# Token DFT of a fused spectral and mixer block: two pairs of row blocks moved from the plain first columns into the first group of the second half, and the first half's results summed in DRAM

## The chip, the cores and the metric

The kernel runs on one core of one Trainium2 chip. The metric is the device time of one execution in microseconds (us). Three runs of the kernel before gave 871.83, 871.90 and 871.99 us, median 871.9 us. TensorE (PE) does the matrix multiplications, VectorE (DVE) and ScalarE (ACT) do elementwise work, GpSimd (POOL) and SyncE (SP) here only issue DMAs, apart from a few small fills.

## What is computed

```python
xn = _layernorm(x, axis=-1)                       # x: 2048 tokens x 640 channels
a = jnp.einsum("bsd,ed->bse", xn, dft_hid_re)
b = jnp.einsum("bsd,ed->bse", xn, dft_hid_im)
y = jnp.einsum("ts,bse->bte", dft_seq_re, a) - jnp.einsum("ts,bse->bte", dft_seq_im, b)
...
h = _layernorm(xn, axis=-1)
u = _gelu(jnp.einsum("bsd,sf->bdf", h, w1) + b1)  # mixed over tokens
return x + y + (jnp.einsum("bdf,fs->bds", u, w2) + b2).transpose(0, 2, 1)
```

The kernel does the DFT over the tokens first and the one over the channels behind it. Everything is in float32.

## The kernel before

**The order of the whole.** There are four stages on PE: the DFT over the tokens, the DFT over the channels ("hid"), and the two matrices of the mixer ("up", "down"). The change is in the first stage, which runs to 403 us in the profile.

**The token DFT.** The 2048 tokens are 16 blocks of 128 rows, k = 0 to 15. The two DFT matrices (m = 0 real, m = 1 imaginary) are read from DRAM in pieces of 128 rows by 512 columns (c = 0 to 3). A matmul takes 128 rows by 128 channels of the normalized x as the stationary operand and a piece of a matrix as the moving one, and sums in one of PE's eight PSUM banks. Float32 accuracy is had from a split: each operand is a high part (`high`, L139, on ACT) and a low part, the rest (`low`, L142, on DVE), and each product is three matmuls (high x high, high x low, low x high; `three`, L150, L151 and L153). The two halves of the split of one piece are called its cut here.

**Plain columns and groups.** The rows come in two halves, h = 0 (blocks 0 to 7) and h = 1 (blocks 8 to 15). The columns c = 0 of the first half are done plainly (`first_columns`, L460): 8 row blocks, 2 matrices, 5 blocks of 128 channels and 3 passes, 240 matmuls on L479. They can start before all rows are there. Every other pair of a half and a column chunk is a group (`columns`, L538), g = 0 to 6: g = 0, 1, 2 are columns 1, 2, 3 of the first half, g = 3 is column 0 of the second half, g = 4, 5, 6 its columns 1, 2, 3. In a group the row blocks are taken in four pairs (q and q + 4), the two matrices and four of the five channel blocks form a 2 by 2 block product, and seven products with sums of the operands take the place of eight (a Strassen scheme); the fifth channel block is done plainly. A pair of row blocks takes 7 x 2 x 3 + 4 x 3 = 54 matmuls in a group and 60 plainly.

**Steps and turns.** The work of PE is a list of steps, each with one piece of a matrix. In a group they come as (product, pair), in the order 1, 2, 5, 6, then 3, 7, 3, 4 with product 3 split in two; products 1, 2, 5 and 3 have 9 matmuls in a step, products 6, 7 and 4 have 6. `turn_of(i)` (L1111) writes out what belongs to step i, and every engine runs its own instructions in that order:

```python
for f in loads.pop(i, ()): ...        # SP: pieces of later steps
for f in reads.pop(i, ()): ...        # PSUM banks read out
steps[j][0]()                         # j = i + 2: high part of a later piece, ACT
extras, timed                         # sums of pieces (DVE), others
do_jobs(ahead, short)
ready[j] = steps[j][1]()              # its low part, DVE
do_jobs(behind)
steps[i][2](ready.pop(i))             # the matmuls of step i, PE
```

So what is put in turn i ahead of a cut delays the cut of step i + 2. There are three places for cut pieces, so that the high part of step j also waits for the matmuls of step j - 3. `jobs` is a list of small pieces of work. How many of them a turn takes, ahead of the low part and behind it, is written out by hand (`JOBS_AT`, by the turn's place in its group).

**The first rows.** The seven products need sums of row pieces. `sums_of_rows` (L299) gives them as six jobs for each pair of the first half: job 1 a sum (L312) and a high part, job 2 a low part, a difference and a high part, job 3 and job 4 the like, job 5 a high part, job 6 a low part. The high parts run on ACT, all else on DVE. The start itself is the string `START` of words: x and b load a row block or a piece, M, A, R, I, F and O make the mean and the factors of a row block (DVE, with one square root on ACT), H and L write the high and low part of its normalized channels (`first_rows`, L343), N normalizes the whole row in place (ACT), T and B are the two halves of a cut, P the matmuls of a step.

**Reading out.** Seven of a group's ten result tiles come in two parts (C11, C12 and C22, two tiles each, and the first F). `fresh` (L601) copies a bank to one of six places "c" on ACT (L604); `more` (L609) later adds a second bank to the copy on DVE (L616); then `store_y` (L454) stores the tile to `y_part` in DRAM from POOL's queue, plainly (L456) in the first half and with an adding DMA (L458) in the second. The plain columns are read on L487.

Of the kernel before, what the change touches and what calls it, by code (L numbers as in the profile page):

```python
# [8 lines left out]
F32 = mybir.dt.float32  # L9
# [5 lines left out]
P = 128  # L15
# [18 lines left out]
BLOCK = 18  # L34


FIRST = (
    [(0, 0, 0, 5), (1, 0, 0, 3), (0, 1, 0, 5), (1, 1, 0, 3)] + [(0, k, 0, 5) for k in range(2, 8)]
    + [(1, k, 0, 5) for k in range(2, 8)] + [(1, 0, 3, 5), (1, 1, 3, 5)]
)  # L40

FIRST_AT = [0, 6, 1, 7, 2, 3, 4, 5, 0, 1, 2, 3, 4, 5, 0, 1, 6, 7]
# [11 lines left out]
GROUP = 28  # L54
# [16 lines left out]
def fnet_plus_mixer(  # L71
# [271 lines left out]
    def first_rows(k, which):  # L343
# [103 lines left out]
    c_turn = [5]  # L447
# [6 lines left out]
    def store_y(h, m, c, j, t):  # L454
        if h == 0:
            nc.gpsimd.dma_start(y_part[m][c][:, j, :], t)  # L456
        else:
            nc.gpsimd.dma_start(y_part[m][c][:, j, :], t, accum_op=ALU.add)  # L458

    def first_columns():  # L460
# [10 lines left out]
        def products(w, m, k, j0, j1, passes=(0, 1, 2)):  # L471

            for n in passes:
                rows, cols = ((0, 0), (0, 1), (1, 0))[n]
                for j in range(j0, j1):
                    begin, end = (2, 1) if m == 1 and j >= 3 else (0, 7)
                    if n == 0 and k == begin:
                        banks[m, j] = psum[(5 * m + j) % 8]
                    nc.tensor.matmul(  # L479
                        banks[m, j], channels(k, j)[rows], w[cols], start=n == 0 and k == begin,  # L480
                        stop=n == 2 and k == end, skip_group_check=True,
                    )

        def read(m, js):
            for j in js:
                c = c_tile()
                nc.scalar.activation(c, banks[m, j], AF.Copy)  # L487
                store_y(0, m, 0, j, c)
# [9 lines left out]
        for i in range(14, 16):  # L498
            loads[i - 6].append(lambda i=i: load(i))

        def row(k):
            if k == 0:
                nc.sync.dma_start(x_in[0][:, :H2], x_rows[0][:, :H2])
            else:
                nc.sync.dma_start(x_in[k], x_rows[k])

# [11 lines left out]
        def rooted(k, to=None):  # L518
            ks = slice(k, (to or k) + 1)
            vq[k] = root(mv[:, ks, 1])  # L520

        def inverted(k, to=None):
            inverse(norm[:, 0, k : (to or k) + 1], *vq[k])

        def factored(k, to=None):
            inverted(k, to)
            offset(norm, slice(k, (to or k) + 1))

        return {
            "x": row, "b": load, "e": later_load, "T": top, "B": bottom, "P": run,  # L530
# [7 lines left out]
    def columns(g, h, c):  # L538

        s0 = len(steps)  # L540
        raw = [pieces[(g + m) % 2] for m in range(2)]
        banks, cs = {}, {}

        def load(name, q):
            i, m = int(name[1]) - 1, int(name[2]) - 1
            nc.sync.dma_start(raw[m][:, i, q, :], dft_seq[m * NC + c, 8 * h + q + 4 * i])

        for name, at in (("B11", (-6, -5, -5, -4)), ("B21", (-3, -3, -2, -2)), ("B12", (-2, -1, 0, 0)), ("B22", (1, 2, 3, 4))):
            for q in range(4):
                loads[s0 + at[q]].append(lambda name=name, q=q: load(name, q))  # L550

        def b(name, q, n=1):
            t = raw[int(name[2]) - 1][:, int(name[1]) - 1]
# [3 lines left out]
        order = [(i, q) for i in (1, 2, 5, 6) for q in range(4)]  # L557
        order += [(3, 0), (3, 1)] + [(7, q) for q in range(4)] + [(3, 2), (3, 3)] + [(4, q) for q in range(4)]
        operand = {1: "B11", 2: "B21", 5: "B11", 6: "B11", 3: "B22", 7: "B12", 4: "B21"}
        for names, at in (  # L560
            (("B11", "B12", "B11"), (5, 7)), (("B12", "B22", "B12"), (6, 8)), (("B11", "B22", "B11"), (9, 11)),
            (("B21", "B21", "B11"), (16, 17)),
        ):
            for e in range(2):
                extras[s0 + at[e]].append(lambda names=names, e=e: sub(*(b(n, 2 * e, 2) for n in names)))
# [8 lines left out]
        def products(i, q):  # L574
            def run(w):
                a = fixed[h][q]
# [3 lines left out]
                if i in fifth_of:  # L580
                    m, low_rows = fifth_of[i]
                    first = q == 0 and i in (1, 2)
                    if first:
# [3 lines left out]
                        first, q == 3,  # L587
                    )
                if i in bank_of:
                    for e in range(2):  # L590
                        at = slot[i] * Q + e * P
                        three(
                            banks[bank_of[i], e], (a[:, 0, at : at + P], a[:, 1, at : at + P]), w,
                            q == 0 and i in (1, 2, 5), q == 3,
# [6 lines left out]
        def fresh(name, at, key, e, then=None):  # L601
            def run():
                cs[name, e] = c_tile()
                nc.scalar.activation(cs[name, e], banks[key, e], AF.Copy)  # L604
                if then:
                    store_y(h, *then, cs[name, e])
            reads[s0 + at].append(run)

        def more(name, at, key, e, then):  # L609
# [580 lines left out]
```

## Time and profile before

| what | value |
|---|---|
| median of three runs | 871.9 us |
| time of the profiled execution | 871.46 us |
| its span, first to last instruction | 869.7 us |
| PE busy | 863.2 us, 99% of the span |
| DVE busy | 698.1 us, 80% |
| ACT busy | 516.7 us, 59% |
| mean granted TensorE clock | 0.999 |

A busy time is the time in which an engine had an instruction under way. In a timeline a row has its start, its duration, the engine, the line of the code, the operation with its tiles ("n" is the fixed parts of the rows, "piece" a cut piece, "pieces" the raw ones, "c" a tile that is read out), a count where several rows are merged, and in brackets the idle time ahead of it with what ended it. Instructions that follow each other on DVE or ACT overlap by about 0.1 us, so that the distance of two starts is what one costs in a busy queue.

### The profile page before, as it was taken

The page shows a single profiled execution, that of the slowest core. Times are in us where ns is not written, and L with a number is a line of the kernel's source. Part 1 is how long each engine was busy: PE and PEld are TensorE (multiplying, and loading weights), DVE is VectorE, ACT ScalarE, POOL GpSimd, SP SyncE. Part 2 cuts the span into 40 slices and gives each one's busy share as a digit, 9 for nine tenths or more (in the row PEclk, how much of TensorE's full clock was granted, in tenths as well). Part 3 has the DMA queues.
Part 4 walks back from the last instruction along what each step waited for, and adds up shares of the span by engine and source line. Part 5 has one row for each costly group of instructions (what it writes and reads, how often), then busy time and mean ns, then how long its engine had stood idle before and what let it go on. Part 6 is the DMA issues. An engine that isn't in the chain of part 4 may idle for free.

```text
span 869.7 us, 13949 instructions
## 1 busy us (share of the span) xinstructions
PE 863.2 (99%) x4908; PEld 791.4 (91%) x4908; DVE 698.1 (80%) x1205; ACT 516.7 (59%) x952; POOL 136.0 (16%) x182
## 2 busy tenths in 40 slices
PE   9999999999999999999999999999999999999997
PEld 6888888888888888889999999999999999999997
DVE  7878878785877887877877788888678978897886
ACT  6654666745455555547565556676677866555653
POOL 0110100101120201222110101111322321111211
PEclk9999999999999999999999999999999999999999
DMA  7670644619383755869576756655588788756776
GB/s 289 232 268 35 206 187 149 256 62 357 51 228 65 177 127 131 215 93 188 131 167 167 159 136 204 188 175 153 154 177 187 166 222 236 181 132 133 165 172 128
DMA packets 87270, 148.95 MB, mean 171 GB/s; under 512 B 8672, under 2 KB 37088, under 8 KB 86944
## 3 DMA queue, kind: packets, MB, share of 16 engines
q1 hardware_dynamic: 64784, 95.64, 34.0%
q0 software_dynamic: 22128, 52.18, 31.1%
q8 instruction: 38, 0.62, 0.3%
q14 instruction: 32, 0.26, 0.1%
q10 hardware_dynamic: 288, 0.25, 0.1%
HBM read 99.96 MB, written 53.31 MB: 176 GB/s over the span
## 4 chain that ended last, share of the span: by engine, by line
PE 99%; DMA 0%; DVE 0%; issue 0%; DVEq 0%; ACT 0%
PE psum L151 31%; PE psum L150 31%; PE psum L153 30%; PE psum L479 6%; DMA x<-in_x 0%; DVE st L211 0%; DVE pair L872 0%; DVE r L229 0%; DVEq L1186 0%; DVE mv L214 0%; ACT q L221 0%; DVE norm L233 0%; DVE r L227 0%; DVE v L220 0%; DVE norm L236 0%
## 5 line engine op out<-in xcount | busy, mean ns | idle before, releaser
L142 DVE TENSOR_TENSOR piece<-pieces,piece 128x512 fp32r<-128x512 f32 (+4 forms) x504 | 332.5, 661 | 135.1 <-ACT piece L139 131.4
L139 ACT ACTIVATE piece<-pieces 128x512 fp32r<-128x512 f32 (+2 forms) x480 | 300.4, 626 | 227.5 <-PE psum L153 148.4
L153 PE MATMUL psum<-piece,n 128*128 128x512 f32 x504 | 196.3, 389 | 0.0
L151 PE MATMUL psum<-piece,n 128*128 128x512 f32 x504 | 196.3, 389 | 0.0
L150 PE MATMUL psum<-piece,n 128*128 128x512 f32 x504 | 196.2, 389 | 0.0
L150 PE MATMUL psum<-sdown,piece 128*128 128x320 f32 x392 | 121.0, 310 | 0.0
L151 PE MATMUL psum<-sdown,piece 128*128 128x320 f32 x392 | 120.9, 309 | 0.0
L151 PE MATMUL psum<-sup,piece 128*128 128x320 f32 x392 | 120.9, 309 | 0.0
L150 PE MATMUL psum<-sup,piece 128*128 128x320 f32 x392 | 120.9, 309 | 0.0
L145 DVE TENSOR_TENSOR pieces<-pieces 128x512 f32<-128x512 f32 (+3 forms) x142 | 111.8, 792 | 2.7
L153 PE MATMUL psum<-sup,piece 128*128 128x320 f32 x368 | 113.9, 309 | 0.0
L153 PE MATMUL psum<-sdown,piece 128*128 128x320 f32 x368 | 113.9, 309 | 0.0
L150 PEld LDWEIGHTS psum<-piece,n 128*128 128x128 f32 x504 | 94.7, 188 | 19.7
L151 PEld LDWEIGHTS psum<-piece,n 128*128 128x128 f32 x504 | 94.6, 188 | 19.7
L153 PEld LDWEIGHTS psum<-piece,n 128*128 128x128 f32 x504 | 94.6, 188 | 19.4
L151 PE MATMUL psum<-shid,piece 128*128 128x320 f32 x280 | 86.6, 309 | 0.0
L150 PE MATMUL psum<-shid,piece 128*128 128x320 f32 x280 | 86.6, 309 | 0.0
L153 PE MATMUL psum<-shid,piece 128*128 128x320 f32 x280 | 86.6, 309 | 0.0
L150 PEld LDWEIGHTS psum<-sdown,piece 128*128 128x128 f32 x392 | 73.6, 188 | 0.2 <-issue 0.2
L151 PEld LDWEIGHTS psum<-sdown,piece 128*128 128x128 f32 x392 | 73.6, 188 | 0.0
L151 PEld LDWEIGHTS psum<-sup,piece 128*128 128x128 f32 x392 | 73.6, 188 | 0.0
L150 PEld LDWEIGHTS psum<-sup,piece 128*128 128x128 f32 x392 | 73.6, 188 | 0.0
(113 smaller groups left out, 1101.8 us busy)
## 6 DMA issues: line engine op xcount, KB each, us to landing
pieces<-in_dft_seq SPq DMA_DIRECT2D x128, 256.0 KB, 5.4
pieces<-in_w SPq DMA_DIRECT2D x88, 256.0 KB, 3.7
y<-c POOLq DMA_DIRECT2D x84, 256.0 KB, 6.5
out<-pair POOLq DMA_DIRECT2D x38, 320.0 KB, 5.2
pieces<-y SPq DMA_DIRECT2D x32, 320.0 KB, 4.1
pieces<-in_w SPq DMA_DIRECT2D x32, 192.0 KB, 2.5
out<-in_x SPq DMA_DIRECT2D x16, 320.0 KB, 7.4
up<-pair POOLq DMA_DIRECT2D x8, 640.0 KB, 3.2
```

The lines of the kernel that those rows point to most:

```text
L139: nc.scalar.activation(hi, src, AF.Copy)
L142: nc.vector.tensor_sub(lo, src, hi.bitcast(F32))
L145: nc.vector.tensor_sub(to, a, b)
L150: nc.tensor.matmul(psum, wh, mh, start=first, stop=False, skip_group_check=True)
L151: nc.tensor.matmul(psum, wh, ml, start=False, stop=last and wl is None, skip_group_check=True)
L153: nc.tensor.matmul(psum, wl, mh, start=False, stop=last, skip_group_check=True)
L479: nc.tensor.matmul(banks[m, j], channels(k, j)[rows], w[cols], start=n == 0 and k == begin, stop=n == 2 and k == end, skip_group_check=True,)
```

## The change

Two pairs of row blocks, (2, 6) and (3, 7), are left out of the plain columns. `FIRST` has 10 steps now, with the blocks 0, 1, 4 and 5; the group of the second half's column 0 (g = 3) takes six pairs, its own four and these two, in 42 steps, the pieces of the two more pairs in a tile of their own ("more"). The row blocks 2, 3, 6 and 7 are still normalized and split, since the groups 0 to 2 need them, but blocks 2 and 3 in fewer channels (`first_rows`), and blocks 6 and 7 partly in the turns 10 to 13.

The results of the first half's groups are no longer added on DVE: both parts are copied on ACT, and the second one is stored with an adding DMA (`by_dram`). That is seven additions a group, for g = 0, 1, 2.

The turns are written out from turn 6 on, where the word list ends. The jobs have a new order and new places: turns 6 and 7 take two jobs each, turns 8 and 9 none, and the 28 turns of the first group up to 23. The mean and variance of the later rows become jobs, and these rows are loaded in turns 10, 14, 18 and 22.

```diff
-BLOCK = 18
+BLOCK = 10
+APART = 2
+FIRST_STEP = 6
...
+FIRST = [
+    (0, 0, 0, 5), (1, 0, 0, 3), (0, 1, 0, 5), (1, 1, 0, 3), (0, 4, 0, 5), (0, 5, 0, 5), (1, 4, 0, 5), (1, 5, 0, 5),
+    (1, 0, 3, 5), (1, 1, 3, 5),
+]
...
 START = """
-    x0 b0 x1 b1 b2 x2 b3 x3 b4 x4 x5 b5 x6 x7 b6 b7
+    x0 b0 x1 b1 b2 x4 b3 x5 b4 x2 x3 b5 x6 x7 b6 b7
     M0 A0 R0 T0 I0 D0 O0 H0 B0 N0 T1 M1 A1 R1 L0 T2 B1 F1 H1 P0-0-1 P1-0 P0-2 P1-1-2
-    M2 A2 R2 N1 B2 F2 L1 b8 T3 H2 M3 A3 B3 N2 T4 R3 P2
-    L2 B4 b9 P3 F3 H3 T5 M4 A4 N3 M5 A5 R4-5 B5 F4-5 L3 b10 e0 P4
-    M6 A6 H4 T6 N4 B6 L4 b11 P5 H5 M7 A7 R6-7 T7 N5 B7 F6-7 L5 b12 e1 P6
-    H6 T8 M8 A8 N6 B8 L6 b13 P7 H7 T9 M12 A12 N7 B9 L7
+    M4 A4 R4 N1 B2 F4 L1 T3 H4 M5 A5 B3 N4 T4 R5 P2
+    L4 B4 P3 F5 H5 T5 M2 A2 N5 M3 A3 R2-3 B5 F2-3 L5 q4 P4
+    H2 T6 N2 M6 A6 B6 L2 q5 P5 H3 T7 N3 M7 A7 R6-7 B7 F6-7 L3
 """
...
 JOBS_AT = (
-    ((0, 1, 2, 3, 4, 10, 13, 15, 18, 19, 20, 21, 22, 23, 26, 27), (0, 1, 2, 3), ()),
-    ((0, 1, 2, 3, 4, 19, 22, 27), (), (10, 14, 21)),
+    jobs_at((0, 1, 2, 4, 10, 12, 13, 14, 15, 16, 17, 18, 23, 25, 27), (2, 4, 10, 15, 16, 16, 17, 17)),
+    jobs_at((0, 1, 2, 3, 4, 10, 12, 13, 14, 15, 18, 19, 20, 21, 22, 23, 26, 27), (0, 1, 2, 3)),
+    jobs_at((0, 1, 2, 41)),
+    jobs_at((0, 1, 2, 3, 4, 13, 18, 19, 22, 27), (), (10, 14, 21)),
 )
...
+        if APART <= k < 4:
+            whole[0] = (lambda which: part(a, which, 0), x_in[k][:, :Q])
...
+            late_begin = 4
+            js = (range(3), range(3, 5)) if (m, k) == (1, late_begin) else (range(j0, j1),)
+            for n, j in ((n, j) for part in js for n in passes for j in part):
...
-        reads[10].append(lambda: read(0, range(ND)))
-        reads[16].append(lambda: read(1, range(3)))
-        reads[18].append(lambda: read(1, range(3, ND)))
+        reads[6].append(lambda: read(0, range(ND)))
+        reads[8].append(lambda: read(1, range(3)))
+        reads[10].append(lambda: read(1, range(3, ND)))
...
+        long = h == 1 and c == 0
+        nq = 4 + (4 - APART) * long
...
+                    more_pairs.append(keep.tile([P, 2, 2, 2, CH], F32, name="more", tag="slab1"))
...
+        order = [(i, q) for i in (1, 2, 5, 6) for q in range(nq)]
+        order += [(3, 0), (3, 1)] + [(7, q) for q in range(nq)] + [(3, q) for q in range(2, nq)]
+        order += [(4, q) for q in range(nq)]
...
-                a = fixed[h][q]
+                a = fixed[h][q] if q < 4 else fixed[0][APART + q - 4]
...
+        by_dram = ("C11", "C12", "C22", "F") if h == 0 else ("C12", "C22") if g == 2 * NC - 2 else ()
...
+        def more(name, when, key, e, then):
+            if name in by_dram:
+                return fresh(name, when, key, e, then, True)
...
+    for q in range(4):
+        loads[BLOCK + 4 * q].append(lambda q=q: later_load(q))
+    for k in (6, 7):
+        at = BLOCK + 2 * (k - 6)
+        extras[at].append(lambda k=k: [start[word](k) for word in "HN"])
+        behind_lo[at + 1].append(lambda k=k: start["L"](k))
+    timed[FIRST_STEP].append(lambda: jobs.extend(first_sums[q][j] for q, j in (
+        (0, 0), (0, 1), (1, 0), (1, 1), (0, 2), (1, 2), (2, 0), (2, 1), (3, 0), (3, 1), (2, 2), (3, 2), (0, 3), (1, 3),
+        (0, 4), (0, 5), (1, 4), (1, 5), (2, 3), (2, 4), (2, 5), (3, 3), (3, 4), (3, 5),
+    )))
...
-        for i in range(8, len(steps) + 1):
-            n_jobs, short = (1, i < BLOCK), False
+        for i in range(FIRST_STEP, len(steps) + 1):
+            n_jobs, short = (i < 8 or i >= BLOCK, i < 8), False
```

More of the change, by code (lines that the diff above doesn't have):

```diff
@@ L471, in products @@
         def products(w, m, k, j0, j1, passes=(0, 1, 2)):
-            for n in passes:
+            late_begin = 4
+            js = (range(3), range(3, 5)) if (m, k) == (1, late_begin) else (range(j0, j1),)
+            for n, j in ((n, j) for part in js for n in passes for j in part):
                 rows, cols = ((0, 0), (0, 1), (1, 0))[n]
[L475 to L482, printed above, removed]
+                begin, end = (late_begin, 1) if m == 1 and j >= 3 else (0, 5)
+                if n == 0 and k == begin:
+                    banks[m, j] = psum[(5 * m + j) % 8]
+                nc.tensor.matmul(
+                    banks[m, j], channels(k, j)[rows], w[cols], start=n == 0 and k == begin,
+                    stop=n == 2 and k == end, skip_group_check=True,
+                )
         def read(m, js):
@@ L505, in row, with begin_loads @@
                 nc.sync.dma_start(x_in[k], x_rows[k])
+        def begin_loads(i):
+            for f in loads.pop(i):
+                f()
         def top(i):
@@ L586, in run @@
                         banks["f", m], (fifth(a, 0, low_rows), fifth(a, 1, low_rows)), w,
-                        first, q == 3,
+                        first, q == nq - 1,
                     )
@@ L605, in run @@
                 if then:
-                    store_y(h, *then, cs[name, e])
-            reads[s0 + at].append(run)
-        def more(name, at, key, e, then):
-            if g == 2 * NC - 2 and name in ("C12", "C22"):
-                return fresh(name, at, key, e, then)
+                    store_y(add, *then, cs[name, e])
+            reads[when].append(run)
+        def more(name, when, key, e, then):
+            if name in by_dram:
+                return fresh(name, when, key, e, then, True)
             def run():
```

133 lines of the change are left out of this document (70 added, 63 removed).

## The prediction

> **What bounds the kernel now.** I read the page first, then what PE waited for, then the chain that ended last, then the groups of instructions.
>
> ```profile
> span 869.7 us, 13949 instructions
> PE 863.2 (99%) x4908; PEld 791.4 (91%) x4908; DVE 698.1 (80%) x1205; ACT 516.7 (59%) x952; POOL 136.0 (16%) x182
> ...
> PE psum L136 <- DVE idle L133: 1.2, 1, 1.2
> PE psum L479 <- DVE norm L236: 0.7, 1, 0.7
> ...
> 6.13 54.90 PE psum L479 x240
> ...
> 60.88 0.39 PE L150 MATMUL psum<-piece,n 128*128 128x512 f32 x1
> ...
> 403.62 0.31 PE L150 MATMUL psum<-shid,piece 128*128 128x320 f32 x1
> ...
> L153 PE MATMUL psum<-piece,n 128*128 128x512 f32 x504 | 196.3, 389 | 0.0
> ```
>
> PE is busy 99% of the span, and its only two waits end before 6.13 us. From there the chain is PE alone. So a matmul left out is time won, at the pace at which matmuls follow each other, and each microsecond in which PE has no cut piece is time lost for good. The pace isn't the 389 ns of the group's row, since matmuls overlap: from the first matmul of the groups (60.88) to the first of the next stage (403.62) there are 342.74 us and 3 x 504 = 1512 matmuls, **0.2267 us each**. The 240 plain ones start at 6.13 and make way for the groups at 60.88.
>
> **Matmuls removed and added.** Plain steps now: (0,0) 15, (1,0) 9, (0,1) 15, (1,1) 9, four of 15, two of 6: 120, so 120 fewer. The long group has 42 steps: 18 of products 1, 2, 5 and 6 of product 3 with 9 matmuls, 18 with 6: 324 in place of 216, so 108 more. Net 12 fewer: 12 x 0.2267 = **-2.72 us**. This part is sure.
>
> **What the plain steps covered.** The 120 plain matmuls that go from the start took 27.2 us there and asked little of the cutters: a plain step has 15 matmuls (3.4 us) for one cut, a group step 9 (2.04 us) or 6 (1.36 us). They covered the first rows and the jobs:
>
> ```profile
> 20.00:40.00 20.00, 20.00 (x90) 16.57 (x89) 17.13 (x50) 14.37 (x28) 2.03 (x4) 1.00 0.62 204
> 40.00:61.00 21.00, 21.00 (x94) 17.40 (x93) 15.56 (x39) 8.98 (x20) 2.42 (x5) 1.00 0.83 277
> ```
>
> (PE, PEld, DVE, ACT, POOL busy in each stretch.) Of the stretch from 40 to 61, where ACT had 8.98 us to do in 21, most is gone. The word list up to P4 has the same kinds of words in the same places with other row numbers, so up to 21.2 us I take the timeline of before as it is. From there ACT, in order, has this to do ahead of the cut of step 10, the first group step:
>
> ```profile
> 6.09 0.98 ACT L260 ACTIVATE n<-x,norm 128x256 fp32r<-128x256 f32 x2 [0.69 <-DVE norm L236]
> ...
> 21.20 1.20 ACT L260 ACTIVATE n<-x,norm 128x512 fp32r<-128x512 f32 x2 [1.07 <-DVE norm L236]
> 22.31 0.62 ACT L139 ACTIVATE piece<-pieces 128x512 fp32r<-128x512 f32 x1
> 22.83 0.91 ACT L260 ACTIVATE x<-x,norm 128x640 f32<-128x640 f32 x1
> 23.65 1.19 ACT L260 ACTIVATE n<-x,norm 128x512 fp32r<-128x512 f32 x2
> 25.95 0.20 ACT L221 ACTIVATE q<-v 128x2 f32<-128x2 f32 x1 [1.11 <-DVE v L220]
> 26.06 0.61 ACT L139 ACTIVATE piece<-pieces 128x512 fp32r<-128x512 f32 x1
> ...
> 37.05 2.56 ACT L487 ACTIVATE c<-psum 128x512 f32<-128x512 f32 x5 [1.86 <-PE psum L479]
> 39.45 0.67 ACT L139 ACTIVATE piece<-pieces 128x512 fp32r<-128x512 f32 x1
> 39.97 0.45 ACT L139 ACTIVATE n<-x 128x256 fp32r<-128x256 f32 x1
> 41.67 0.42 ACT L139 ACTIVATE n<-x 128x256 fp32r<-128x256 f32 x1 [1.25 <-DVE x L145]
> 41.99 0.62 ACT L139 ACTIVATE piece<-pieces 128x512 fp32r<-128x512 f32 x1
> ...
> 57.45 1.57 ACT L487 ACTIVATE c<-psum 128x512 f32<-128x512 f32 x3 [1.49 <-PE psum L479]
> 58.90 0.65 ACT L139 ACTIVATE piece<-pieces 128x512 fp32r<-128x512 f32 x1
> ...
> 59.57 0.69 DVE L142 TENSOR_TENSOR piece<-pieces,piece 128x512 fp32r<-128x512 f32 x1 [2.20 <-ACT piece L139]
> ```
>
> The distance of two starts is what each costs. H2 (256 and 128 channels, the pair of 0.98 less 0.09 of overlap) 0.89; T6 0.52; N2 0.82; H3 0.89; T7 0.52; N3 0.82; the square root 0.11: 25.77 us. Then turn 6: five copies of the first sums, 37.05 to 39.45, 2.40: 28.17. The cut of step 8 with two jobs, whose difference on DVE stands between two high parts on ACT, 39.45 to 41.99, 2.54: 30.71. Turn 7, cut and two jobs, again 2.54: 33.25. Turn 8: three copies, 57.45 to 58.90, 1.45: 34.70. The high part of step 10, and 0.67 later (58.90 to 59.57) the low part, 0.69: 36.06. PE needs that low part for the second matmul of step 10, the 122nd of all. In before that place was at 60.88 - 120 x 0.2267 + 0.23 = 33.9. So PE comes there **+2.15 us** late. None of these ACT entries waits for PE: step 5 is through at 60.88 - 162 x 0.2267 = 24.2, and step 7 by 31.5. Inside this lies a smaller stall in step 6 (the five copies free the bank of its tenth matmul at 26.4 where PE asks at 26.2, the next bank 0.5 later), which isn't added. Bounds: with the jobs of both turns at the bare distance of their ACT rows (0.52 + 2 x 0.32 in place of 2.54) it is 2.15 - 2.76, so nothing is lost; with 0.25 more at each of four hand-offs it is 3.15. I stay with the row that is the same turn with the same jobs.
>
> **The first group.** It has 20 of the 24 jobs, the words H, N and L of blocks 6 and 7 and 28 cuts in 49 us.
>
> ```profile
> L142 DVE TENSOR_TENSOR piece<-pieces,piece 128x512 fp32r<-128x512 f32 x362 | 249.2, 689 | 112.9 <-ACT piece L139 110.6 <-DMA later<-in_x 0.8
> L139 ACT ACTIVATE piece<-pieces 128x512 fp32r<-128x512 f32 x362 | 227.4, 629 | 174.3 <-PE psum L153 124.5 <-DVE piece L142 22.6 <-DVE c L616 7.0
> L145 DVE TENSOR_TENSOR pieces<-pieces 128x1024 f32<-128x1024 f32 x28 | 34.1, 1219 | 0.0
> L604 ACT ACTIVATE c<-psum 128x512 f32<-128x512 f32 x74 | 42.6, 591 | 6.6 <-PE psum L153 4.7
> L616 DVE TENSOR_TENSOR c<-psum,c 128x512 f32<-128x512 f32 x45 | 30.8, 684 | 0.0
> ...
> 41.55 0.88 DVE L211 BATCH_NORM_STATS2 st<-later 128x6 f32<-128x320 f32 x2
> ...
> 43.82 0.42 DVE L142 TENSOR_TENSOR n<-x,n 128x256 fp32r<-128x256 f32 x1
> 44.15 0.42 DVE L145 TENSOR_TENSOR x<-x 128x256 f32<-128x256 f32 x1
> ```
>
> With each mean less its overlap, DVE has 28 x 0.61 for cuts, 8 x 1.14 for sums, 26 x 0.34 for the jobs' operations, 2 x 0.8 for L of blocks 6 and 7 and 3 x 1.05 for moments: 40 of 49 us. ACT has 28 x 0.52 + 17 x 0.49 for cuts and copies, 4 for H and N (as above) and 12 x 0.33 for the jobs: 31. Both fit on average; I followed the queue for the places where they don't. Behind the late step 10 the high parts of block 6 and 7 (turns 10, 12) and the jobs of turns 12 and 14 keep ACT busy until the cut of step 17, whose low part is 0.1 late: **+0.1**. At step 26 ACT copies C12 as step 25 ends; then four cuts, six jobs and a sum of two pieces (1.14) lie in a row before the low part of step 31: 0.2 + 0.47 + 0.67 + 4 to 5 us of alternating jobs and cuts + 1.14 + 0.69 = 8.85 us behind the start of step 26, where PE wants it at 36 x 0.2267 + 0.23 = 8.39: **+0.4**, bounds 0 (every hand-off at 0.35 in place of 0.45) and 1.5.
>
> **The additions moved.** 21 additions leave DVE (0.68 each) for ACT (0.59); they stand behind product steps with 9 matmuls or run before the bank that the cut's own wait brings, so nothing on PE's path: cover, the two steps that a cut is ahead. The C22 and C12 copies of offsets 22 to 25 cost ACT 0.49 each ahead of cuts that have 0.7 to 2 us of slack; gone, that cover costs at most 0.5 a group. The adding stores:
>
> ```profile
> L458 POOL DMA_DIRECT2D y<-c x44: 842/855/1529, 228.7 to 405.6; - x44
> DMA to landing us min/median/max: 3.8/7.0/10.1
> ...
> L456 POOL DMA_DIRECT2D y<-c x40: 539/539/710, 38.0 to 208.9; - x40
> DMA to landing us min/median/max: 2.3/6.1/8.3
> ```
>
> Seven more a group at 0.86 us on POOL, which has 5.4 us of work in a group of 49. An adding store waits on POOL for the landing of the plain store to the same place; behind it are other stores, and behind these the copies into the six "c" places. The nearest two parts (F, turns 4 and 10 of the group) are 12 us apart, the landing at most 8.3. A place is written again after 9.5 us at the least (turns 10 to 16), the stores before it land after about 8; a wait of 1 us there is inside the slack of a 9-matmul step. I take 0, bounds 0 and 1. The Trainium skill ("DMA: Bandwidth & Descriptors", Rules for kernel authors) says that an accumulating DMA must wait for the semaphore of an earlier DMA on the same bytes, which speaks against summing in DRAM; by it the 21 waits are due here too, and by the landings above they have ended before POOL comes to them, so the sum stays.
>
> **Second half.** The long group's 12 sums and 42 cuts on DVE (42 x 0.61 + 12 x 1.14 + 7 x 0.6 = 44 of 73 us) fit; its first piece in "more" waits for step 25 of group 2, and lands some 5 to 8 us later where PE asks 10.9 us later. The end of the kernel is unchanged. 0.
>
> **Sum.** -2.72 + 2.15 + 0.1 + 0.4 = -0.1 us on the span of 869.7. The profiled execution took 871.46, 1.76 outside the span, and stands 0.44 below the median; so 871.9 - 0.1 = **871.8 us**. A measurement of this kernel tells about 0.2% (1.7 us) from no change.
>
> **Rivals.** *The cover holds* (chance 0.16): ACT and DVE interleave better than the row of turn 10 says, PE is hardly late, and 2.72 less up to 1 us is won: 869.2 to 870.1. For it: no plain step of before waits for a cut after 6.13. Against: the ACT entries are strictly in order, and 13.5 us of them fill 21.2 to 34.7. *Hand-offs decide* (0.18, slower): in the runs of 6-matmul steps of the first group each job passes from ACT to DVE and back; from 0.2 us more at each of about ten such passes, on top of the sum, it is slower by 0.2%, and at 0.3 us more (3 us) it gives 874.8. For it: the longest waits of ACT for such a difference were 1.25 us; against: DVE is free for 9 of the 49 us. *The clock falls* is part of neither:
>
> ```profile
> 2.07 0.15 PEld L136 LDWEIGHTS <-idle 128*128 128x128 bf16 x1 [0.28 <-issue]
> 2.49 0.15 PEld L136 LDWEIGHTS <-idle 128*128 128x128 bf16 x1 [0.28 <-issue]
> ...
> 4.19 0.75 PEld L136 LDWEIGHTS <-idle 128*128 128x128 bf16 x4 [0.27 <-issue]
> ```
>
> At the start matmuls came 0.42 us apart, and 0.20 apart from 4.2 us on; were PE so slow again after its stall at step 10, for the same 3 us, 7 matmuls would lose 0.2 us each, +1.4: 873.2 (0.04, inside the range). The Trainium skill ("TensorE: Matmul & The Clock Gate", Part 1) says that the clock halves only after an idle window of about 3.4 us; the stall of 1.7 us is shorter, and the 0.7 us wait at 6.13 did nothing to the granted clock of 1.00.
>
> **Chances.** My forecast with the clock's case 0.66, its own range 870.4 to 873.6 (the bounds of step 10 and 31 in part, since all high ends together are unlikely). The cover's rival is taken into the range, the upper one is left out from 873.8 on: 869.2 to 873.8. Faster by over 0.2% is the first rival, 0.16; slower the second, 0.18; within, 0.66.
>
> **What would show it.** L479 x120 and 540 in each of L150, L151 and L153 for 128x512: the -2.72. A wait of PE on a cut piece of 1.5 to 2 us near 34 to 36 us, with the ACT copies of L487 (x3) and both jobs' high parts ahead of it: the +2.15; no such wait: the cover's rival. Waits of PE on "piece" between 60 and 76 us: the hand-offs. Waits of ACT's L604 rows on a DMA, or of PE beyond 85 us, would make the part on the stores wrong. A first group matmul after 36.5 us or several waits over 0.5 us make the forecast too low.

## The result and the profile after

The changed kernel takes **873.93 us**, median of 11 runs (873.84 to 875.06); the kernel before took 871.83 us in 11 runs beside it (871.50 to 872.19). The ratio is 1.0024, 95% interval 1.0016 to 1.0033: slower by 2.1 us, where the prediction said 871.8 and at most 873.8. The page of the changed kernel and what PE waited for (us in total, times, longest):

```profile
span 872.4 us, 13964 instructions
...
PE 862.4 (99%) x4896; PEld 788.6 (90%) x4896; DVE 692.8 (79%) x1194; ACT 528.9 (61%) x979; POOL 154.6 (18%) x203
```

```profile
PE psum L490 <- DVE norm L242: 1.3, 1, 1.3
...
PE psum L156 <- ACT piece L145: 0.8, 1, 0.8
PE psum L157 <- DVE piece L148: 0.2, 1, 0.2
```

PE has the 12 matmuls less (4896), and two waits that it had not. (Line numbers of the changed kernel are 6 to 49 higher: low parts L148, high parts L145, matmuls L156, L157 and L159, plain ones L490, their copies L498, the group's copies L642.) That view names only waits that it can put down to an engine. The timeline of PE shows more. Matmuls start 0.227 us apart; each wider step is time lost:

```profile
25.79 2.50 PE L490 MATMUL psum<-piece,n 128*128 128x512 f32 x8
...
34.05 0.84 PE L490 MATMUL psum<-piece,n 128*128 128x512 f32 x3
35.71 0.49 PE L156 MATMUL psum<-piece,n 128*128 128x512 f32 x1 [0.81 <-ACT piece L145]
36.44 0.50 PE L157 MATMUL psum<-piece,n 128*128 128x512 f32 x1 [0.23 <-DVE piece L148]
36.77 0.40 PE L159 MATMUL psum<-piece,n 128*128 128x512 f32 x1
...
50.63 0.39 PE L156 MATMUL psum<-piece,n 128*128 128x512 f32 x1
51.14 0.50 PE L157 MATMUL psum<-piece,n 128*128 128x512 f32 x1
51.47 0.40 PE L159 MATMUL psum<-piece,n 128*128 128x512 f32 x1
...
74.88 0.39 PE L156 MATMUL psum<-piece,n 128*128 128x512 f32 x1
75.25 0.50 PE L157 MATMUL psum<-piece,n 128*128 128x512 f32 x1
...
98.29 0.39 PE L156 MATMUL psum<-piece,n 128*128 128x512 f32 x1
98.75 0.50 PE L157 MATMUL psum<-piece,n 128*128 128x512 f32 x1
```

The first row lies around step 6: eight matmuls at the pace would take 1.98 us. The others are step 10 (its first matmul waits for the high part, its second for the low one), step 17, step 31, and, in the second group, its step 6. By the starts of all matmuls in the trace, the time lost over the pace is 0.50 us in step 6 (before 28 us), 1.59 in step 10, 0.40 in step 17, 0.26 in step 31 and 0.35 in the second group: 3.10 us against the 2.72 that the missing matmuls give. Slips of less than 0.04 us each, most of them just behind these places, make another 0.17. From the first plain matmul to the first hid matmul it takes 398.04 us in place of 397.49, 0.55 more.

From there to the last matmul both kernels take 461.2 us. Behind it they differ again (times from the last matmul to the end are counted from that matmul's start). POOL's draining is the longest of its DRAIN instructions at the program's end; it starts with POOL's last store. Here are that store and the draining (count; shortest, median and longest ns; first and last start of the DRAINs), before and after, by the timeline and by the source line of the program's end:

```profile
861.76 0.48 DVE L867 TENSOR_TENSOR pair<-psum,pair 128x320 f32<-128x320 f32 x1
862.28 0.73 DVE L142 TENSOR_TENSOR piece<-pieces,piece 64x128 fp32r<-64x128 f32 x2
862.54 0.85 POOL L1021 DMA_DIRECT2D out<-pair  x1 [4.34 <-DVE pair L867]
```

```profile
L1186 POOLq DRAIN  x3: 40/102/6281, 862.5 to 869.3; - x3
```

```profile
862.80 0.48 DVE L906 TENSOR_TENSOR pair<-psum,pair 128x320 f32<-128x320 f32 x1
863.32 0.73 DVE L148 TENSOR_TENSOR piece<-pieces,piece 64x128 fp32r<-64x128 f32 x2
864.32 0.85 POOL L1060 DMA_DIRECT2D out<-pair  x1 [5.08 <-DVE piece L148]
```

```profile
L1235 SPq DRAIN  x3: 7/7/7, 869.3 to 871.9; - x3
...
L1235 POOLq DRAIN  x3: 40/102/7343, 864.3 to 872.2; - x3
```

The store carries DVE's sum of 862.80, which ends at 863.28. In the kernel before, it left POOL 0.30 us behind that sum (861.76), now 1.04 us behind it. POOL's draining takes 7.34 us in place of 6.28; it ends at 871.6, when SP has long been done (869.3), and the program ends with it. The store is 0.74 us later and the draining 1.06 longer, and what follows the draining takes 0.1 less: from the last matmul to the end it is 6.56 us in place of 4.86, **+1.70**. So the span is longer by 0.55 on PE, 1.70 at the end and 0.48 at the start, and the start turns out to be chance.

### The profile page after: what moved, and what is told of

The parts are those of the page before. It is cut to its first block, busy times and chain, and to the rows that moved or that the text cites. A ratio compares the mean times of both kernels' runs of the same rounds, so it can differ in the third digit from the quotient of the medians.

```text
span 872.4 us, 13964 instructions
## 1 busy us (share of the span) xinstructions
PE 862.4 (99%) x4896; PEld 788.6 (90%) x4896; DVE 692.8 (79%) x1194; ACT 528.9 (61%) x979; POOL 154.6 (18%) x203
## 4 chain that ended last, share of the span: by engine, by line
PE 91%; ACT 3%; DVE 2%; DMA 2%; issue 1%; DVEq 0%; ACTq 0%
PE psum L157 31%; PE psum L156 31%; PE psum L159 30%; DMA pieces<-in_dft_seq 2%; DVE piece L148 1%; ACT piece L145 1%; ACT n L266 1%; DVE st L217 0%; ACT c L498 0%; ACT x L266 0%; DVE n L148 0%; DMA x<-in_x 0%; ACT c L642 0%; ACT n L145 0%; DVE r L235 0%
## 5 line engine op out<-in xcount | busy, mean ns | idle before, releaser
L148 DVE TENSOR_TENSOR piece<-pieces,piece 128x512 fp32r<-128x512 f32 (+4 forms) x496 | 326.1, 659 | 135.7 <-ACT piece L145 132.7
L145 ACT ACTIVATE piece<-pieces 128x512 fp32r<-128x512 f32 (+2 forms) x472 | 294.7, 626 | 202.6 <-PE psum L159 126.6
L156 PE MATMUL psum<-piece,n 128*128 128x512 f32 x540 | 210.2, 389 | 0.8 <-ACT piece L145 0.8
L157 PE MATMUL psum<-piece,n 128*128 128x512 f32 x540 | 210.5, 390 | 0.4 <-DVE piece L148 0.2
L159 PE MATMUL psum<-piece,n 128*128 128x512 f32 x540 | 210.1, 389 | 0.0
L157 PEld LDWEIGHTS psum<-piece,n 128*128 128x128 f32 x540 | 101.3, 188 | 23.0 <-DVE piece L148 2.0
L156 PEld LDWEIGHTS psum<-piece,n 128*128 128x128 f32 x540 | 101.4, 188 | 22.2 <-ACT piece L145 1.2
L156 PE MATMUL psum<-sdown,piece 128*128 128x320 f32 x392 | 120.9, 309 | 0.0
L157 PE MATMUL psum<-sdown,piece 128*128 128x320 f32 x392 | 120.8, 309 | 0.0
L157 PE MATMUL psum<-sup,piece 128*128 128x320 f32 x392 | 120.8, 309 | 0.0
L156 PE MATMUL psum<-sup,piece 128*128 128x320 f32 x392 | 120.8, 309 | 0.0
L159 PEld LDWEIGHTS psum<-piece,n 128*128 128x128 f32 x540 | 101.4, 188 | 21.1
L159 PE MATMUL psum<-sup,piece 128*128 128x320 f32 x368 | 113.7, 309 | 0.0
L159 PE MATMUL psum<-sdown,piece 128*128 128x320 f32 x368 | 113.7, 309 | 0.0
L467 POOL DMA_DIRECT2D y<-c x65 | 56.0, 911 | 251.0 <-DVE c L653 157.0
L159 PE MATMUL psum<-shid,piece 128*128 128x320 f32 x280 | 86.5, 309 | 0.0
L157 PE MATMUL psum<-shid,piece 128*128 128x320 f32 x280 | 86.5, 309 | 0.0
L156 PE MATMUL psum<-shid,piece 128*128 128x320 f32 x280 | 86.5, 309 | 0.0
L919 ACT ACTIVATE pair<-psum 128x320 f32<-128x320 f32 x101 | 44.1, 436 | 50.3 <-PE psum L159 47.4
L156 PEld LDWEIGHTS psum<-sdown,piece 128*128 128x128 f32 x392 | 73.6, 188 | 0.2 <-issue 0.2
L156 PEld LDWEIGHTS psum<-sup,piece 128*128 128x128 f32 x392 | 73.6, 188 | 0.0
```

The costliest lines, as they stand in the source:

```text
L145: nc.scalar.activation(hi, src, AF.Copy)
L148: nc.vector.tensor_sub(lo, src, hi.bitcast(F32))
L156: nc.tensor.matmul(psum, wh, mh, start=first, stop=False, skip_group_check=True)
L157: nc.tensor.matmul(psum, wh, ml, start=False, stop=last and wl is None, skip_group_check=True)
L159: nc.tensor.matmul(psum, wl, mh, start=False, stop=last, skip_group_check=True)
L919: nc.scalar.activation(c, b, AF.Copy)
```

## Experiments

The theory after the two traces: the greater part of the loss sits at the end and comes from POOL's 21 more stores; the rest is PE's loss up to 100 us, which ACT's queue with its hand-offs sets. The main rivals: the end and the start vary by execution; the regrouped half, not the stores, makes the end late; DVE's chain sets the waits. Times below are medians beside runs of the kernel before on the same chip (871.8 to 871.9).

**c_before and c_after: both kernels again, as they are.**

> The kernel before once more, for its two ends. In the first profiles the changed kernel's first plain matmul came at 6.62 us in place of 6.13 and its span ended 6.5 us behind the last matmul's start in place of 4.9. If these are chance of one execution, this one shows either value (first matmul 6.1 to 6.7, tail 4.9 to 6.6). If they belong to the kernels, it shows 6.13 and 4.9 again, span 869.7.

> The changed kernel once more. Theory 1 (PE waits for cut pieces): the same five late places, PE 3.6 us late in all behind the first matmul, at 36.4, 51.1, 75.3 and 98.8 us, moved by the time of the first matmul. Theory 2 (the two ends): span 872.2 again with a tail of 6.5 us if the tail belongs to the kernel; a tail of 4.9 and a span of 870.7 if it was chance.

Measured: the first plain matmul at 6.56 (before) and 6.29 us (after), the other way round than first; from there to the first hid matmul 397.55 and 398.08; from the last matmul to the end 4.86 and 6.53. The start is chance, PE's 0.5 us and the 1.7 us at the end belong to the kernel. (From the first hid matmul to the last one, c_before took 461.7 us where the other three executions took 461.2, so half a microsecond there can be chance, too.)

**j_order: the first four jobs in another order.**

```diff
-        (0, 0), (0, 1), (1, 0), (1, 1), (0, 2), (1, 2),
+        (0, 0), (1, 0), (0, 1), (1, 1), (0, 2), (1, 2),
```

> The changed kernel with the jobs (0,1) and (1,0) in each other's place: the same work in turns 6 and 7, but in turn 6 no high part waits for a difference of the same turn. Theory 1, the hand-offs hold ACT ahead of step 10: the three copies of turn 8 start 1.2 us earlier, PE's wait at step 10 is 1.2 us shorter, the span 0.8 to 1.2 us shorter (872.2 to 871.2). Rival, ACT is full until step 17 anyway: step 10 comes earlier, but the wait at step 17 grows by the same and the span stays within 0.3 us.

Measured 873.67 us, ratio 1.0021 (1.0012 to 1.0030). From the first plain to the first hid matmul 397.60: 0.44 less than the changed kernel, half of what I expected. In turn 6 ACT now waits 0.79 us for a sum in place of 1.25 for a difference; turn 7 keeps its 1.24. Step 17 didn't get worse. So the hand-offs do count, at what they leave ACT idle, and this order takes only one of them away.

**adds_dve: the first half's additions back on DVE.**

```diff
-        by_dram = ("C11", "C12", "C22", "F") if h == 0 else ("C12", "C22") if g == 2 * NC - 2 else ()
+        by_dram = ("C12", "C22") if g == 2 * NC - 2 else ()
```

(`fresh` and `more` store plainly in the first half again.)

> The changed kernel with the first half's second parts added on DVE and stored plainly, as before: the moved pairs alone. Theory 1: the additions cost nothing where they stand, and the copies neither; the waits of PE stay as they are but for those at 75 and 99 us, the time within 0.7 us of the changed kernel. Rival, the copies and adding stores are what costs: 2 us less, 871.9.

Measured 881.58 us, ratio 1.0107 (1.0093 to 1.0121). This time says nothing on the additions, for PE has a wait that no other run has:

```profile
PE psum L156 <- ACT pair L919: 6.4, 1, 6.4
```

With 84 copies in place of 105 the ring of six places ends in the other half of them, the first hid step takes its place just where the last stores still run, and PE waits 6.4 us behind 404 us. The end, though, was 4.7 us. Hence the same again with the ring begun elsewhere; there the wait is gone:

**adds_dve2: the moved pairs alone** (`c_turn = [5]`).

> The changed kernel with the first half's additions back on DVE and the six places of the copies begun so that the last copy lies as in the kernel before: the moved pairs alone. Theory A: 175 stores on POOL, so the end is 5.0 us as before; PE's waits up to the first hid matmul stay within 0.5 us of the changed kernel's (398.05 from the first plain matmul): 872.2 us, and no wait of 6.4 us for a bank behind 404 us. Rival (the additions on DVE lie in the way of the cuts of the first group): 1 to 2 us more wait there, 873.5.

Measured 872.88 us, ratio 1.0017 (1.0008 to 1.0026), 0.7 above what theory A gave; its runs spread from 872.3 to 876.9, and the profiled one took 872.44. The end is 4.74 us, so with 175 stores it is as before: theory A. PE needs 398.34 from the first plain to the first hid matmul, 0.3 more than the changed kernel (one more wait, 0.16 in all, at 64 us, and 0.11 more in the second group): the moved additions gave PE back that little.

**before_dram: the stores without the moved pairs.** In the kernel before, `by_dram` for the first half as in the changed one, with the 21 copies on ACT that belong to it (and the ring of six places begun as there, `c_turn = [2]`):

```diff
+        by_dram = ("C11", "C12", "C22", "F") if h == 0 else ("C12", "C22") if g == 2 * NC - 2 else ()
...
-            if g == 2 * NC - 2 and name in ("C12", "C22"):
-                return fresh(name, at, key, e, then)
+            if name in by_dram:
+                return fresh(name, at, key, e, then, True)
```

> The kernel before with one part of the change alone: the first half's additions are copies on ACT and adding stores on POOL (21 more stores, 196 in all, as in the changed kernel). Theory A (the late end belongs to the place of a store in POOL's sequence: the 196th waits about 1 us after its release): the pace of PE is as before (within 0.5 us from the first plain matmul to the first hid matmul, 397.5), and from the last matmul to the end of the span it takes 6.6 us in place of 5.0: 873.4 us. Theory B (the late end comes with the moved pairs and the regrouped half, not with the stores): the end stays 5.0 us, 871.8. Theory C (a fetch of DVE's instructions, which in the changed kernel came 2.7 us ahead of the last matmul, holds POOL up): DVE has 21 fewer instructions here, the fetch falls elsewhere, the end stays 5.0.

Measured **873.97 us**, ratio 1.0027 (1.0017 to 1.0037). Timeline and source line:

```profile
863.93 0.86 POOL L1024 DMA_DIRECT2D out<-pair  x1 [5.08 <-DVE piece L142]
```

```profile
L1189 POOLq DRAIN  x3: 40/93/7337, 863.9 to 871.7; - x3
```

The same late store and the same long draining without any moved pair: 6.66 us from the last matmul to the end. PE lost 0.3 us (397.82). With adds_dve2 this decides it: the 21 stores cost 1.7 to 1.8 us at the end, with the moved pairs and without them. The third theory in the expectation, a fetch of DVE's instructions, wanted an end of 5.0 us here and of 6.6 in the next run, b_pool; both came otherwise.

**b_pool and pool_190: other numbers of stores on POOL.** One load more, or six plain stores less:

```diff
-    loads[s_hid + 20].append(lambda: nc.sync.dma_start(b1_sb, b1))
+    loads[s_hid + 20].append(lambda: nc.gpsimd.dma_start(b1_sb, b1))
```

> The changed kernel with one small load (b1, 3.5 KB) issued by POOL in place of SP, about 450 us ahead of the end: POOL's last store is its 197th. Theory A (place in POOL's sequence): the 196th is now the last but one, which nobody waits for; the last starts 0.3 us after its release, the end is 5.0 us, the time 872.2. Theory C (DVE's instruction fetch): DVE's instructions are the same, the end stays 6.6 us and the time 873.9. If the delay hangs on the kind of data alone, also 6.6.

```diff
-        if not add:
+        if not add and m == 0 and j in (2, 3) and c > 0:
+            nc.sync.dma_start(y_part[m][c][:, j, :], t)
+        elif not add:
             nc.gpsimd.dma_start(y_part[m][c][:, j, :], t)
```

> The changed kernel with six plain stores of the first half issued by SP in place of POOL, so that POOL issues 190 in all and its last is the 190th. If the delay of 0.74 us at the start belongs to the 196th store, it goes; if POOL's longer draining at the end (7.3 us from its last issue in place of 6.3) comes with the 196th too, the end is 5.0 us and the time 872.2; if it comes with more stores than the 175 of before, 5.8 and 873.1; if neither hangs on their number, 6.6 and 873.9.

Measured 873.21 us (ratio 1.0017, 1.0008 to 1.0026) and 873.04 us (1.0015, 1.0006 to 1.0024); the end is 5.73 and 5.43 us, where the expectations had 5.0 or 6.6 for b_pool, and 5.0, 5.8 or 6.6 for pool_190. b_pool, then pool_190:

```profile
858.78 0.85 POOL L969 DMA_DIRECT2D out<-pair  x1 [0.38 <-issue]
863.62 0.85 POOL L1060 DMA_DIRECT2D out<-pair  x1 [3.99 <-DVE pair L906]
```

```profile
L1235 POOLq DRAIN  x3: 46/93/7262, 863.6 to 871.4; - x3
```

```profile
L1237 POOLq DRAIN  x3: 40/102/6960, 863.2 to 870.7; - x3
```

In both the last store is on time again (b_pool's leaves 0.3 us behind its sum). In b_pool the last but one is now the 196th; measured back from the last matmul it leaves 0.70 us later than in the changed kernel, without harm to anyone. So the 0.74 us belong to a place in POOL's sequence. The traces show more such places, where nobody waits: the 80th transfer (0.9 us late) in the kernels with 175 to 197 but pool_190, there the 77th (0.86), and the 114th in the changed kernel and in pool_190 (1.3). It isn't the number alone, then, and what makes such a place is open.

The draining is another matter: 6.28, 6.96, 7.34 and 7.26 us with 175, 190, 196 and 197 transfers. The traces part it in two. The last store lands 3.4 to 3.6 us after it was issued, and from this landing to the draining's end it takes 2.82, 3.48, 3.72 and 3.76 us, the same to 0.01 us in every trace with 175 and in every one with 196 transfers: some **0.044 us for each**. The one transfer that b_pool has more is 3.5 KB and costs 0.04 like a store of 256 KB, adding or plain, so by this one load it is the number that counts and not the bytes. I had expected only one rule for both; theory A was right on the number and wrong in taking the two for one.

**n_later: ACT relieved ahead of step 10.**

```diff
-    H2 T6 N2 M6 A6 B6 L2 q5 P5 H3 T7 N3 M7 A7 R6-7 B7 F6-7 L3
+    H2 T6 M6 A6 B6 L2 q5 P5 H3 T7 M7 A7 R6-7 B7 F6-7 L3
...
+    extras[9].append(lambda: [start['N'](k) for k in (2, 3)])
```

In this kernel the low parts of rows 2 and 3 (L2, L3) are taken ahead of N2 and N3, from rows not yet normalized; the instructions are the same in number and size.

> The changed kernel with the high parts of rows 2 and 3 (2 x 0.82 us on ACT) taken out of the list ahead of step 10 and put behind step 9's cut, so ACT has 1.6 us less ahead of step 10. My theory (ACT's queue in order sets PE's wait at step 10): the waits at 35.7 to 36.8 us (0.87 together over the pace, with the restart) go to nothing, and as ACT has the same work up to step 17, the wait at 51 us grows by no more than what step 10 won: between -0.9 and 0 us, 873.0 to 873.9. Rival (the jobs' hand-offs between ACT and DVE set it): the wait stays within 0.3 us.

Measured 876.09 us, ratio 1.0045 (1.0032 to 1.0058), outside both ranges. Step 10 kept its wait, and between 42 and 53 us PE lost 1.9 us, where the changed kernel loses 0.4. (Another 0.56 us were lost behind the first hid matmul; as c_before shows, that may be chance.) Two things follow. What is put behind step 10 comes back as waits in steps 13 to 17, so ACT is full there. And the five copies came only 0.28 us earlier (25.92), for the square root ahead of them had to wait for DVE's variance:

```profile
25.81 0.20 ACT L227 ACTIVATE q<-v 128x2 f32<-128x2 f32 x1 [1.27 <-DVE v L226]
```

Ahead of the copies ACT's own work and DVE's chain end at nearly the same time, so taking ACT's alone off wins almost nothing.

**n_fill: the same work in the gaps of the hand-offs.**

```diff
-    H2 T6 N2 M6 A6 B6 L2 q5 P5 H3 T7 N3 M7 A7 R6-7 B7 F6-7 L3
+    H2 T6 M6 A6 B6 q5 P5 H3 T7 M7 A7 B7
...
+    behind_lo[6].append(lambda: start["N"](2))
+    extras[7].append(lambda: (start["L"](2), start["R"](6, 7)))
+    behind_lo[7].append(lambda: start["N"](3))
+    extras[8].append(lambda: (start["L"](3), start["F"](6, 7)))
```

> The changed kernel with the fifths of rows 2 and 3 (N, ACT 0.82 us each), their low parts and the factors of rows 6 and 7 moved from the list's end into turns 6 to 8, where ACT stands idle 1.25 us at a hand-off of each turn. The same work, nothing left out. My theory (what lies on ACT in order ahead of step 10, with its hand-offs, makes PE late in steps 6 and 10): the five copies start at 24.6 us in place of 26.2, PE's 0.50 us lost in step 6 goes to nothing, the 1.59 us at step 10 falls to 0 to 0.5; step 17 may lose up to 0.3 more: 872.0 to 872.8 us (the late end of 6.6 us stays). Rival (DVE's own chain of the two turns sets the low part of step 10): the copies are earlier, but step 10 keeps 1.2 to 1.6: 873.3.

Measured 872.33 us, ratio 1.0006 (0.9997 to 1.0014), 1.6 us less than the changed kernel. First ACT in the changed kernel, then in this one (timeline):

```profile
25.29 0.91 ACT L266 ACTIVATE x<-x,norm 128x640 f32<-128x640 f32 x1
26.10 0.19 ACT L227 ACTIVATE q<-v 128x2 f32<-128x2 f32 x1
26.20 2.50 ACT L498 ACTIVATE c<-psum 128x512 f32<-128x512 f32 x5
28.59 0.63 ACT L145 ACTIVATE piece<-pieces 128x512 fp32r<-128x512 f32 x1
...
30.77 0.42 ACT L145 ACTIVATE n<-x 128x256 fp32r<-128x256 f32 x1 [1.25 <-DVE x L151]
...
33.26 0.42 ACT L145 ACTIVATE n<-x 128x256 fp32r<-128x256 f32 x1 [1.25 <-DVE x L151]
33.58 1.55 ACT L498 ACTIVATE c<-psum 128x512 f32<-128x512 f32 x3
35.02 1.16 ACT L145 ACTIVATE piece<-pieces 128x512 fp32r<-128x512 f32 x2
```

```profile
24.15 2.50 ACT L498 ACTIVATE c<-psum 128x512 f32<-128x512 f32 x5
...
27.36 0.93 ACT L266 ACTIVATE x<-x,norm 128x640 f32<-128x640 f32 x1
28.73 0.42 ACT L145 ACTIVATE n<-x 128x256 fp32r<-128x256 f32 x1 [0.44 <-DVE x L151]
...
31.23 0.42 ACT L145 ACTIVATE n<-x 128x256 fp32r<-128x256 f32 x1 [0.32 <-DVE x L151]
31.55 1.55 ACT L498 ACTIVATE c<-psum 128x512 f32<-128x512 f32 x3
32.98 1.16 ACT L145 ACTIVATE piece<-pieces 128x512 fp32r<-128x512 f32 x2
```

The two activations of 0.9 us now fill ACT's two gaps of 1.25. The square root (`R`) has moved behind the copies as well, so that they don't wait for DVE's variance as in n_later. The copies start 2.05 us earlier, the cut of step 10 too (0.34 of it is this execution's earlier first matmul). Step 6 loses nothing more, step 10 0.5 us in place of 1.59, step 17 the same 0.4. PE needs 396.36 us, 1.68 less.

**best1: n_fill with the additions on DVE and one job of the second group later.** It has the edits of n_fill and adds_dve2 and one more. In the second group the two normalizations of later rows stood on ACT ahead of the copies and so of its step 6's cut (first rows below, changed kernel). Without the 3 in the second list the job falls into turn 4, behind the cut (last rows, best1):

```diff
-    jobs_at((0, 1, 2, 3, 4, 10, 12, 13, 14, 15, 18, 19, 20, 21, 22, 23, 26, 27), (0, 1, 2, 3)),
+    jobs_at((0, 1, 2, 3, 4, 10, 11, 12, 13, 14, 15, 18, 19, 20, 21, 22, 23, 26, 27), (0, 1, 2)),
```

> The same as the run n_fill, with the additions on DVE as in adds_dve2 (175 stores on POOL) and one job of the second group later by one turn, so that the two activations of 0.87 us on the later rows no longer lie ahead of the cut of its step 6. Theory: adds_dve2's 872.3 less 1.5 to 2.0 of steps 6 and 10 and less 0.45 of the second group: 870.0 to 870.6 us, the end 5.0 us. Rival (waits only pass on to the next turn): 871.8 to 872.3.

```profile
94.75 1.74 ACT L266 ACTIVATE later<-later,norm 128x640 f32<-128x640 f32 x2 [0.59 <-DVE norm L242]
96.39 1.06 ACT L642 ACTIVATE c<-psum 128x512 f32<-128x512 f32 x2
97.34 0.62 ACT L145 ACTIVATE piece<-pieces 128x512 fp32r<-128x512 f32 x1
```

```profile
92.61 1.07 ACT L642 ACTIVATE c<-psum 128x512 f32<-128x512 f32 x2
93.56 0.63 ACT L145 ACTIVATE piece<-pieces 128x512 fp32r<-128x512 f32 x1
94.08 1.73 ACT L266 ACTIVATE later<-later,norm 128x640 f32<-128x640 f32 x2
```

Measured **870.35 us**, ratio 0.9982 (0.9973 to 0.9991): faster than both kernels. The loss in the second group is gone, the end is 4.81 us, PE needs 396.17.

**best2: best1 with fewer transfers on POOL and one job more moved.**

```diff
-        if not add:
+        if not add and c > 0:
+            nc.sync.dma_start(y_part[m][c][:, j, :], t)
+        elif not add:
...
-    jobs_at((0, 1, 2, 4, 10, 12, 13, 14, 15, 16, 17, 18, 23, 25, 27), (2, 4, 10, 15, 16, 16, 17, 17)),
+    jobs_at((0, 1, 2, 4, 6, 10, 12, 13, 14, 15, 16, 17, 18, 23, 25, 27), (2, 10, 15, 16, 16, 17, 17)),
```

> The kernel of the run best1 with two more edits, which the profile tells apart by place. (1) The 30 plain stores of the first half's groups go by SP, so POOL issues 145. From 175, 190 and 196 stores POOL's draining at the end took 6.3, 7.0 and 7.3 us, 0.05 us for each store; so 4.85 us here, and the time from the last matmul to the end falls from 4.8 to 3.7 us (SP's own end, 2.8 us behind the last matmul, is next). Rival (the draining hangs on the bytes or on the adding stores, not on the number): it stays 6.3, end 4.8. (2) The second job behind step 4 of the first group goes ahead of step 6: its hand-off of 0.95 us no longer stands ahead of the cut of step 17, and PE's 0.40 us lost there go. Rival (ACT is full there, the wait only moves): 0.4 stays, in step 17 or the steps up to 21. Together 870.35 - 1.1 - 0.4 = 868.9 us; 870.0 to 870.4 by both rivals; loads that come late behind SP's stores would show as waits of ACT on a DMA, and could cost 1 us.

```profile
L1241 POOLq DRAIN  x3: 40/102/5024, 860.9 to 866.8; - x3
```

Measured **868.87 us**, ratio 0.9962 (0.9948 to 0.9976), as forecast. With 145 transfers the draining takes 5.02 us (4.85 forecast), of it 1.48 behind the last store's landing, 30 x 0.045 less than with 175; the end is 3.82. Step 17 loses nothing, PE needs 395.69. By the trace SP now ends its own work 0.3 us later than POOL's draining, so by this estimate still fewer transfers on POOL would win nothing.

## Why the prediction was wrong

**The failed step** is the one on the tail: "The end of the kernel is unchanged. 0." With it fell the price of the adding stores ("I take 0, bounds 0 and 1"). I had followed them where they stand, up to the places and landings in the groups, and there the bounds hold: before_dram lost 0.3 us on PE. But they are charged once more, at the end, where POOL drains 0.044 us longer for each transfer it has issued (21 make 0.9; the last store's slower landing adds 0.16) and where the last store happened to become the 196th (0.74). That is 1.7 of the 2.1 us. That this store fell on a late place is bad luck, but the draining alone would have made the end 0.9 us later. The profile of before had the hint, and the prediction does not use it: 4.9 us behind the last matmul, and POOL's draining of 6.28 us in the view of the last source line.

**Matmuls removed: right.** 120 on L490, 540 on each of the three lines, 2.72 us.

**Step 10: right.** Late by 2.15 us, predicted with a smaller stall in step 6 inside; measured 0.50 in step 6 and 1.59 in step 10, 2.09. The first pass of the queue was right in its times, too: copies from 25.77 predicted, 26.20 measured; low part ready at 36.06 predicted, PE's second matmul at 36.44; and 0.49 us of each difference is the later first matmul. What it had wrong is the reason at one place: the copies would not have come earlier with less ACT work alone, since DVE's variance was due at about the same time (n_later).

**Steps 17 and 31: mis-sized.** 0.1 and 0.4 predicted, 0.40 and 0.26 measured. The 0.4 does not come out of its own terms: as written they add up to 7.2 to 8.2 us, not to 8.85, and so to less than the 8.39 at which PE comes; by them step 31 would not wait at all. That the 0.4 lay near the 0.26 is luck. Step 17 hung on one hand-off of 0.95 us ahead of a copy and a cut; with that job elsewhere it is gone (best2).

**The second group: not looked at.** I took the sum of work in the first group (40 of 49 us) and followed its queue, but the moments and factors of the later rows, now jobs, end in the second, and its step 6 lost 0.35 us. The prediction had named PE waits beyond 85 us as a sign against its part on the stores; the wait came, but not from them: before_dram lost only 0.1 there at 91 us, and adds_dve2, without the stores, lost 0.45 at the same step. On PE the sum was -0.1 and the measurement +0.55: 0.3 of the difference is step 17, 0.35 the second group, 0.17 the small slips, less 0.2 by which steps 10 and 31 came out smaller.

**The rivals.** *The cover holds*: no, the waits of steps 6 and 10 are there. *Hand-offs decide* (slower by 0.2%): the sign came, the reason didn't; behind step 10 the first group lost 0.66 us, where that rival wanted 2 to 3 more than the sum. *The clock falls*: the granted clock stayed at 1.00. By the Trainium skill ("TensorE: Matmul & The Clock Gate", Part 1) a stall as short as this one leaves the clock alone; the rows agree, only one matmul behind each wait came 0.11 us late (36.44 to 36.77 where 0.227 is the pace).

**Did DVE hold the late store up?** The late store left POOL 0.27 us behind the end of a low part on DVE (864.05). The Trainium skill ("SBUF — State Buffer", the section on SBUF's two separate sides) says that some operations of DVE lock POOL out of a shared port, so that it can't write the descriptors of a transfer. If the low part were such an operation, it could have held the store up. But in before and in b_pool the store of the same sum goes out beside the same low part (862.54 beside 862.28 to 863.01 in before, rows above), and whether it does went with its place in POOL's sequence. So the low part is not the cause, and the lateness of that place stays unexplained.

## What to carry to other kernels

A transfer on POOL was paid twice here: where it is issued, and again in the draining at the end, which was on the critical path; count an engine's transfers when work is moved to it, and open the profile's view of the program's last line. The Trainium skill ("DMA: Bandwidth & Descriptors", Issuing engine by pattern) gives plain loads and stores to SP and calls that path generally faster; here 30 plain stores moved there took 1.0 us off the end. Before an in-order queue is called the bound, look for its gaps: two activations put into two gaps of 1.25 us, with the square root moved out of the copies' way, won 1.6 us; put behind step 9's cut, with the square root left where it was, the same two made the kernel 2.2 us slower.

## What the runs showed of the hardware

- POOL's draining at the end of the program took 5.02, 6.28, 6.96, 7.34 and 7.26 us with 145, 175, 190, 196 and 197 transfers issued by POOL. Counted from the landing of the last store it is 1.48, 2.82, 3.48, 3.72 and 3.76 us, 0.044 us for each transfer, plain or adding, of 256 KB or of 3.5.
- Some places in POOL's sequence start a transfer late, the 196th by 0.74 us, the same to 0.02 us in each of the six traces where it is the last. What makes these places was not found.
- At each of five places one matmul behind a wait started 0.11 us late. Why was not found.
- The first plain matmul started between 6.13 and 6.62 us in different executions, in both kernels, 2.6 us behind the landing of the first row block's load in each.
